# Hash by full-height block-diagonal matmuls, and separate PSUM banks for preparation and output rows

## The chip, the cores and the metric

The kernel runs on one core of one Trainium2 chip. The metric is the device time of one execution in microseconds. The core's engines appear in the profile as PE (TensorE matmuls), PEld (TensorE weight loads), DVE (VectorE), ACT (ScalarE), POOL (GpSimd) and SP (SyncE, which issues transfers). Each engine works through its own instructions in order and waits on semaphores for the others. TensorE writes its results to PSUM, from where VectorE or ScalarE takes them to SBUF.

## The reference

Hash attention comes first, then a gated feed-forward layer with a residual. With batch 4, 8 heads, 768 tokens and a head size of 64:

```python
q_bits = (q @ proj > 0)            # proj is 64 x 6: six bits for each token and head
k_bits = (k @ proj > 0)
mask = bucket(q_bits) == bucket(k_bits)      # a query sees only keys of its bucket
scores = where(mask, q @ k.T / 8, -1e9)
attn = softmax(scores) ;  a = attn @ v

x = a as (4 * 768) tokens x 512
g = x @ w_gate ;  val = x @ w_val            # 512 -> 1536
ffn = (gelu(g) * val) @ w_out                # 1536 -> 512
out = x + sigmoid(x @ w_res) * ffn
```

## The kernel before

Heads are handled in pairs, sixteen of them, and each pair has nine chunks ("slots") of scores. The mask is folded into the scores' matmul: each query and key gets seven more rows, its six bits as plus or minus one half and a constant, and the product of these rows is zero where the buckets agree and a large negative number where they differ. So the hash bits have to be laid out as rows (`bits`), and small transfers (`mask_rows`) put them under the transposed queries and keys (`aug` for the first head of a pair, `second` for the other).

The PSUM pools and the constants of the hash:

```python
    sc_ps = ctx.enter_context(tc.tile_pool(name="sc_ps", bufs=2, space=PSUM))
    av_ps = ctx.enter_context(tc.tile_pool(name="av_ps", bufs=1, space=PSUM))
    mm_ps = ctx.enter_context(tc.tile_pool(name="mm_ps", bufs=1, space=PSUM))
# ... cut ...
    projw = const.tile([P, 2, 32], FP32, name="projw")
    nc.vector.memset(projw, 0.0)
    for a in range(4):
        nc.scalar.dma_start(projw[32 * a:32 * a + 32, :, 0:NBITS],
                            proj.rearrange("(h r) n -> r h n", r=32))
# ... cut: cst, the value that each bit row adds after the comparison ...
```

The hash works on 32x32 blocks (`t32`, transposed by VectorE). A row group `a` of 32 partitions is a tile of the array of its own; one call takes two of the four row groups, for all tensors (`jobs`) of two pairs:

```python
    def hash_mm(jobs, a0, ps=mm_ps, tag="mm"):

        while rows_open:
            mlp_piece()
        hs = ps.tile([P, 2, 512], FP32, tag=tag, name="hs")
        for dh in range(2):
            for j, x in enumerate(jobs):
                for i in range(2):
                    a = a0 + i
                    nc.tensor.matmul(hs[32 * j:32 * j + 32, i, 0:HT * 32],
                                     projw[32 * a:32 * a + 32, dh, :],
                                     t32[x][32 * a:32 * a + 32, :, dh, :],
                                     start=(dh == 0), stop=(dh == 1),
                                     tile_position=(32 * a, 32 * j))
        hsum[a0] = hs
        if a0 == 2:
            for x in jobs:
                del t32[x]

    def hash_bits(jobs, a0):
        n = 32 * len(jobs)
        if a0 == 0:
            bits[jobs[0]] = bit_pool.tile([P, HT, P], BF16, tag="bits", name="bits")
        dst = bits[jobs[0]].rearrange("p c (a n) -> p a c n", a=4)[:n, a0:a0 + 2]
        hs = hsum.pop(a0)[:n, :, 0:HT * 32].rearrange("p a (c n) -> p a c n", c=HT)
        nc.vector.tensor_scalar(dst, hs, 0.0, cst[:n], op0=ALU.is_gt, op1=ALU.add)

    def mask_rows(jobs, xs, eng=nc.sync):
        for j, x in enumerate(jobs):
            if x not in xs:
                continue
            for h, dst in ((1, second[x[0] % NM][x[1]][0:NROW]), (0, aug[x][D:D + NROW])):
                eng.dma_start(dst, bits[jobs[0]][32 * j:32 * j + NROW, h * T:(h + 1) * T])
```

Transposition of queries and keys on TensorE, both sides of a pair in one PSUM tile:

```python
    def transpose_pe(p):
        tp = mm_ps.tile([P, 2, 1024], BF16, tag="mm", name="tp")
        for side in range(2):
            n = nats.pop((p, side)).rearrange("p t h d -> p t (h d)")
            for t in range(T):
                nc.tensor.transpose(tp[:, side, t * P:(t + 1) * P], n[:, t, :], ident)
        tps[p] = tp

    def transposed(x, eng):
        src = tps[x[0]][:, x[1], 0:S]
        dst = new_aug(x).rearrange("p t n -> p (t n)")
        if eng is nc.scalar:
            nc.scalar.copy(dst, src)
        else:
            eng.tensor_copy(dst, src)
```

Values, and the end of a pair. `x_transpose` puts the finished pair into the layout that the feed-forward part reads; it uses TensorE for the first batch and for the last pair of every batch:

```python
    def finish(p):
        b, hp = divmod(p, HP)
        if hp == 0:
            x_tok[b] = x_pool.tile([P, HP, T, 2 * D], BF16, tag="x_tok", name="x_tok")
            x_sb[b] = x_pool.tile([P, HP, T, P], BF16, tag="x_sb", name="x_sb")
        o = av.pop(p)[:, :, 0:T * (D + 1)].rearrange("p h (t d) -> p h t d", t=T)
        rec = sm_pool.tile([P, 2, T], FP32, tag="rec", name="rec")
        nc.vector.reciprocal(rec, o[:, :, :, D])
        nc.vector.tensor_mul(x_tok[b][:, hp].rearrange("p t (h d) -> p h t d", h=2),
                             o[:, :, :, 0:D],
                             rec.unsqueeze(3).to_broadcast([P, 2, T, D]))

    def x_transpose(p):
        b, hp = divmod(p, HP)
        xt = x_tok[b][:, hp]
        if b == 0 or hp == HP - 1:
            while rows_open:
                mlp_piece()
            tp = mm_ps.tile([P, T, P], BF16, tag="mm", name="tp")
            for t in range(T):
                nc.tensor.transpose(tp[:, t, :], xt[:, t, :], ident)
            nc.vector.tensor_copy(x_sb[b][:, hp], tp)
        else:
            nc.sync.dma_start_transpose(out=x_sb[b][:, hp], in_=xt.rearrange("p t n -> p (t n)"))
# ... cut ...
    def values(p, c, e):
        va, vsum = vaug[p]
        if c == 0:
            av[p] = av_ps.tile([P, 2, 512], FP32, tag="av", name="av")
        for hi in range(2):
            o = av[p][:, hi, 0:T * (D + 1)].rearrange("p (t d) -> p t d", t=T)
            if c == 0:
                nc.tensor.matmul(
                    o, eps_sb,
                    vsum[:, hi, 0:D + 1].unsqueeze(1).to_broadcast([P, T, D + 1]),
# ... cut ...
    def flush():
        while pending:
            values(*pending.pop(0))

    def scores(p, c):
        ops = ((D + NROW, aug[p, 0], aug[p, 1]), (P, *second[p % NM]))
        sp = sc_ps.tile([P, 1024], FP32, tag="sp", name="sp")
        for hi, (n, qs, ks) in enumerate(ops):
            off = hi * 512
            for (jt, qt0, nq) in chunks[c]:
                nc.tensor.matmul(sp[:, off:off + nq * P], ks[0:n, jt, :],
                                 qs[0:n, qt0:qt0 + nq, :], start=True, stop=True)
                off += nq * P
        e = e_pool.tile([P, 1024], BF16, tag="e", name="e")
        nc.scalar.activation(e, sp, AF.Exp, scale=float(ALPHA))
        return (p, c, e)
```

Output rows. `rps` (the residual's gate) and `fps` (the feed-forward output) are two halves of one tile of `mm_ps`. It is a generator: each `yield` is the end of a piece that the main loop places between attention slots.

```python
    def project(b, pools=((mm_ps, "mm"),)):

        hh = hidden.pop(b)
        for t in range(T):
            ps, tag = pools[t % len(pools)]
            acc = ps.tile([P, 2, DMODEL], FP32, tag=tag, name="acc")
            rps, fps = acc[:, 0, :], acc[:, 1, :]
            for kk in range(KM):
                nc.tensor.matmul(rps, x_sb[b][:, kk, t, :], wr[:, kk, :],
                                 start=(kk == 0), stop=(kk == KM - 1))
            th = g_pool.tile([P, DMODEL], FP32, tag="th", name="th")
            nc.scalar.activation(th, rps, AF.Tanh, scale=0.5)
            rows_open.append(t)
            yield
            for m in range(KF):
                nc.tensor.matmul(fps, hh[:, m, bass.ts(t, P)], wo[:, m, :],
                                 start=(m == 0), stop=(m == KF - 1))
                if m % 3 == 2 and m < KF - 1:
                    yield
            o = o_pool.tile([P, DMODEL], FP32, tag="o", name="o")
            nc.vector.scalar_tensor_tensor(o, th, 1.0, fps, op0=ALU.add, op1=ALU.mult)
            o3 = o.rearrange("p (k n) -> p k n", k=KM)
            nc.vector.scalar_tensor_tensor(o3, o3, 0.5, x_tok[b][:, :, t, :],
                                           op0=ALU.mult, op1=ALU.add)
            nc.sync.dma_start(out_t[b, t], o)
            rows_open.pop()
            yield
```

The preamble, the schedule of preparation and the main loop:

```python
    jobs0, jobs1 = pair_jobs(0), pair_jobs(1)
    warm_up(8)
    cast((0, 0), nc.scalar)
    cast((0, 1), nc.gpsimd)
    blocks((0, 0))
    blocks((0, 1))
    transpose_pe(0)
    hash_mm(jobs0, 0, sc_ps, "sp")
    hash_mm(jobs0, 2, sc_ps, "sp")
    transposed((0, 0), nc.scalar)
    transposed((0, 1), nc.scalar)
    hash_bits(jobs0, 0)
    hash_bits(jobs0, 2)
    for x in jobs0:
        move_second(x, nc.gpsimd)
    mask_rows(jobs0, jobs0[:1])
    mask_rows(jobs0, jobs0[1:], nc.scalar)
# ... cut: loads, casts, values of pair 0, blocks of pair 1 ...
    at(0, transpose_pe, 1)
    at(0, transposed, (1, 0), nc.vector)
    at(0, transposed, (1, 1), nc.vector)
    at(2, hash_mm, jobs1, 0)
    at(2, move_second, (1, 0), nc.gpsimd)
    at(2, move_second, (1, 1), nc.gpsimd)
    at(2, hash_bits, jobs1, 0)
    at(3, hash_mm, jobs1, 2)
    at(3, hash_bits, jobs1, 2)
    at(3, mask_rows, jobs1, jobs1)
    at(3, values_cast, 1)
    at(3, values_sum, 1)
    at(3, load, 2, (2,))

    for g in range(1, NPAIR // 2):
        s0 = 18 * (g - 1) + (3 if g == 1 else 0)
        pa, pb = 2 * g, 2 * g + 1
        jobs = pair_jobs(pa, pb)
        for i, x in enumerate(jobs):
            at(s0 + 2 * (i // 2), cast, x, nc.gpsimd)
            at(s0 + 1 + i, blocks, x)
        for i, p in enumerate((pa, pb)):
            s1 = s0 + 2 + 3 * i
            if g < 3:
                at(s1, transpose_pe, p)
                for side in range(2):
                    at(s1, transposed, (p, side), nc.vector)
                    at(s1 + 2 + side, move_second, (p, side), nc.gpsimd)
            else:
                for side in range(2):
                    at(s1, transpose_dma, (p, side))
                    at(s1 + 5 + side, move_second, (p, side), nc.gpsimd)
        at(s0 + 8, hash_mm, jobs, 0)
        at(s0 + 8, hash_bits, jobs, 0)
        at(s0 + 10, hash_mm, jobs, 2)
        at(s0 + 10, hash_bits, jobs, 2)
        at(s0 + 11, mask_rows, jobs, jobs[:2])
        at(s0 + 14, mask_rows, jobs, jobs[2:])
        at(s0 + 4, values_cast, pa)
        at(s0 + 4, values_sum, pa)
        at(s0 + 9, values_cast, pb)
        at(s0 + 9, values_sum, pb)
        at(s0 + 5, load, pb, (2,))
        if g + 1 < NPAIR // 2:
            at(s0 + 4, load, pa + 2, (0, 1))
            at(s0 + 6, load, pb + 2, (0, 1))
            at(s0 + 10, load, pa + 2, (2,))
# ... cut: weight loads ...
    LEAD = 5
    HELD = 6
    for s in range(NSLOT):
        p, c = divmod(s, NCH)
        b, slot = divmod(s, NCH * HP)
        new = scores(p, c)
        for f in tasks[s]:
            f()
        if b >= 1:
            if slot < LEAD:
                mlp_piece()
                mlp_piece()
            elif mlp and mlp[0][1] < 5 * T - HELD:
                mlp_piece()
        flush()
        pending.append(new)
        if c == 1 and p >= 1:
            x_transpose(p - 1)
        if b >= 1 and slot == LEAD - 1:
            while mlp:
                mlp_piece()
            gate_val(b - 1)
            mlp.append([project(b - 1), 0])
    flush()
    x_transpose(NPAIR - 1)
    while mlp:
        mlp_piece()
    gate_val(B - 1)
    for _ in project(B - 1, ((mm_ps, "mm"), (av_ps, "av"))):
        pass
```

Of the kernel before, what the change touches and what calls it, by code (L numbers as in the profile page):

```python
# [17 lines left out]
def kernel(  # L18
# [25 lines left out]
    assert D == 64 and S == 768 and NROW <= 32 and HP == KM  # L44
# [29 lines left out]
    mm_ps = ctx.enter_context(tc.tile_pool(name="mm_ps", bufs=1, space=PSUM))  # L74
# [24 lines left out]

    projw = const.tile([P, 2, 32], FP32, name="projw")  # L100
    nc.vector.memset(projw, 0.0)
    for a in range(4):
        nc.scalar.dma_start(projw[32 * a:32 * a + 32, :, 0:NBITS],
                            proj.rearrange("(h r) n -> r h n", r=32))
# [4 lines left out]


    cst = const.tile([P, 1], FP32, name="cst")
    nc.gpsimd.memset(cst, -0.5)
    for j in range(4):
        nc.gpsimd.affine_select(
            out=cst, in_=cst, compare_op=ALU.not_equal,
            fill=(1.0 if j % 2 == 0 else -NBITS / 4.0),
            base=-(32 * j + NBITS), pattern=[[0, 1]], channel_multiplier=1)
# [3 lines left out]
                            base=0, pattern=[[-1, P]], channel_multiplier=1)  # L121

# [27 lines left out]
    wps = av_ps.tile([P, 512], FP32, tag="av", name="wps")  # L150

    def warm_up(n):
        for _ in range(n):
            nc.tensor.matmul(wps, eps_sb, warm, start=True, stop=True)
# [28 lines left out]
    def transpose_pe(p):  # L183
        tp = mm_ps.tile([P, 2, 1024], BF16, tag="mm", name="tp")
        for side in range(2):
            n = nats.pop((p, side)).rearrange("p t h d -> p t (h d)")
            for t in range(T):
                nc.tensor.transpose(tp[:, side, t * P:(t + 1) * P], n[:, t, :], ident)
        tps[p] = tp

    def transposed(x, eng):
        src = tps[x[0]][:, x[1], 0:S]
        dst = new_aug(x).rearrange("p t n -> p (t n)")
        if eng is nc.scalar:
            nc.scalar.copy(dst, src)
        else:
            eng.tensor_copy(dst, src)
# [7 lines left out]
    mlp, rows_open = [], []  # L205
# [11 lines left out]
    def hash_mm(jobs, a0, ps=mm_ps, tag="mm"):  # L217

        while rows_open:
            mlp_piece()  # L220
        hs = ps.tile([P, 2, 512], FP32, tag=tag, name="hs")
        for dh in range(2):
            for j, x in enumerate(jobs):
                for i in range(2):
                    a = a0 + i
                    nc.tensor.matmul(hs[32 * j:32 * j + 32, i, 0:HT * 32],  # L226
# [321 lines left out]
```

## Time and profile before

| | |
|---|---|
| time, median of 2 runs | 434.26 us (432.81 to 435.72) |
| profiled run | 430.43 us, span 428.6 us, granted TensorE clock 0.982 |
| exp on ScalarE (L339) | 144 of 1022 ns |
| hash matmuls on TensorE (L226) | 512 records, 27.7 us busy |
| bits on VectorE (L242) | 18, 18.2 us busy |
| output rows on TensorE (L375, L382) | 25.4 and 72.6 us busy |
| gate and value projections (L354) | 125.5 us busy |

The span begins with a preamble that ends with the first score matmul at 15.65 us. Attention alone follows (the first batch), then four times a stage of gate and value projections (L354), and between them stages in which the next batch's attention is mixed with the output rows of the batch before. The last 28 us are the output rows of the last batch. A group in the profile is named by line, engine and tile: `acc` is the rows' PSUM tile, `hs` the hash sums, `tp` transposes, `sp` scores, `av` the values' output, `e` the exponentials, `th` the tanh, `o` the output row in SBUF. "idle before" is the time in which the engine stood still ahead of that group and what ended it. FP32 matmuls are recorded as two passes each.

### The profile page before, as it was taken

Reading aid. Unit: us, or ns where it says so; the run is one execution under the profiler, and the core shown is the slowest. Engines: PE = TensorE matmul, PEld = TensorE weight load, DVE = VectorE, ACT = ScalarE, POOL = GpSimd, SP = SyncE. Lnnn points to the kernel's source line nnn. Section 1 sums busy time; section 2 is a strip of 40 time slices with the busy share of each in tenths; the row PEclk is TensorE's granted clock in tenths of the full one; section 3 lists DMA queues with packets and bytes.
Section 4 is the critical chain, followed back from the end, with each engine's and each line's share of the span. In section 5 each row is a group of like instructions: output and inputs, shape, how many; then the busy total and the mean of one; then the engine's idle time right before and its main releaser. Section 6 shows DMA issues by size and latency. Waiting matters only on the chain. (4 is left out here: it accounts for less than half of the span.)

```text
span 428.6 us, 7961 instructions
## 1 busy us (share of the span) xinstructions
PE 367.1 (86%) x3301; PEld 202.5 (47%) x3360; DVE 154.1 (36%) x201; ACT 208.6 (49%) x227; POOL 108.1 (25%) x187
## 2 busy tenths in 40 slices
PE   7688788999789887999779988999869976999884
PEld 3354544665335444566335544566435543566431
DVE  3472634333232434433331543433241212333232
ACT  3366768335327765533537765633626784233110
POOL 4969596133011154250002145230000000000000
PEclk9999999999799999999999999999998998999999
DMA  7343989980030590900012490700020100000011
GB/s 257 116 139 131 263 125 192 213 192 0 26 84 29 132 255 24 262 4 2 24 55 60 111 274 8 136 0 2 2 65 29 52 18 26 24 2 0 26 63 59
DMA packets 47299, 37.32 MB, mean 87 GB/s; under 512 B 25312, under 2 KB 44192, under 8 KB 47264
## 3 DMA queue, kind: packets, MB, share of 16 engines
q1 hardware_dynamic: 40308, 31.15, 26.4%
q0 software_dynamic: 6336, 5.24, 8.3%
q8 instruction: 26, 0.43, 0.4%
q10 hardware_dynamic: 620, 0.42, 0.3%
q14 instruction: 9, 0.07, 0.1%
HBM read 29.37 MB, written 6.29 MB: 83 GB/s over the span
## 5 line engine op out<-in xcount | busy, mean ns | idle before, releaser
L339 ACT ACTIVATE e<-sp 128x1024 bf16<-128x1024 f32 x144 | 143.7, 1022 | 66.9 <-PE sp L335 58.5
L382 PE MATMUL acc<-wo,hh 128*128 128x512 bf16 x275 | 72.6, 388 | 9.5 <-ACT th L378 8.4
L360 ACT ACTIVATE gt<-sp 128x768 bf16<-128x768 f32 x48 | 38.9, 810 | 82.4 <-PE sp L354 82.3
L316 PEld LDWEIGHTS <-e 128*128 128x128 bf16 x1152 | 51.8, 98 | 54.7 <-ACT e L339 34.9
L363 DVE TENSOR_TENSOR hh<-gt,sp 128x768 bf16<-128x768 bf16 x48 | 45.8, 955 | 82.0 <-PE sp L354 82.0
L316 PE MATMUL av<-va,e 128*128 128x65 bf16 x1152 | 62.3, 195 | 13.4 <-ACT e L339 12.3
L354 PE MATMUL sp<-x_sb,wg 128*128 128x256 bf16 (+1 forms) x378 | 69.9, 325 | 0.3
L354 PE MATMUL sp<-x_sb,wv 128*128 128x512 bf16 (+1 forms) x374 | 69.7, 324 | 0.5
L335 PE MATMUL sp<-aug,aug 71*128 71x512 bf16 x192 | 55.6, 330 | 4.5 <-DMA aug<-bits 4.5
L382 PEld LDWEIGHTS <-hh 128*128 128x128 bf16 x288 | 28.4, 99 | 44.0 <-issue 17.8
L354 PEld LDWEIGHTS <-wg 128*128 128x128 bf16 x384 | 37.3, 98 | 25.0 <-issue 0.5
L354 PEld LDWEIGHTS <-wv 128*128 128x128 bf16 x384 | 37.4, 98 | 24.4
L335 PE MATMUL sp<-second,second 128*128 128x256 bf16 (+1 forms) x171 | 47.5, 323 | 0.0
L387 DVE SCALAR_TENSOR_TENSOR o<-th,acc 128x512 f32<-128x512 f32 x24 | 16.4, 684 | 79.4 <-PE acc L382 60.8
L179 POOL COPY second<-aug 64x768 bf16<-64x768 bf16 x32 | 25.8, 826 | 66.3 <-DMA aug<-nat 57.9
L378 ACT ACTIVATE th<-acc 128x512 f32<-128x512 f32 x24 | 14.3, 596 | 57.7 <-PE acc L375 57.4
L254 POOL CAST va<-ldv 128x768 bf16<-128x768 f32 x16 | 13.2, 827 | 101.4 <-DMA ldv<-in_v_dram 74.1
L226 PE MATMUL hs<-t,projw 32*32 32x384 f32 x512 | 27.7, 509 | 7.9 <-DVE o L387 6.7
L375 PE MATMUL acc<-wr,x_sb 128*128 128x512 bf16 x88 | 25.4, 393 | 9.5 <-DVE bits L242 7.0
L284 DVE RECIPROCAL rec<-av 128x12 f32<-128x12 f32 x16 | 3.7, 232 | 75.6 <-PE av L316 75.6
L201 DVE STREAM_TRANSPOSE t<-ld 128x768 f32<-128x768 f32 x32 | 29.3, 952 | 2.2 <-DMA ld<-in_q_dram 2.2
L242 DVE TENSOR_SCALAR bits<-hs,cst 128x768 bf16<-128x768 f32 (+1 forms) x18 | 18.2, 1015 | 23.5 <-PE hs L226 23.5
(45 smaller groups left out, 219.9 us busy)
## 6 DMA issues: line engine op xcount, KB each, us to landing
ld<-in_q_dram SPq DMA_DIRECT2D x16, 384.0 KB
ldv<-in_v_dram SPq DMA_DIRECT2D x16, 384.0 KB
out_dram<-o SPq DMA_DIRECT2D x24, 256.0 KB
ld<-in_k_dram SPq DMA_DIRECT2D x15, 384.0 KB
wg<-in_moe_w_gate_dram POOLq DMA_DIRECT2D x4, 384.0 KB, 5.7
wv<-in_moe_w_val_dram POOLq DMA_DIRECT2D x4, 384.0 KB, 7.0
wo<-in_moe_w_out_dram POOLq DMA_DIRECT2D x3, 512.0 KB, 17.8
wr<-in_moe_w_res_dram POOLq DMA_DIRECT2D x1, 512.0 KB, 11.1
```

Of the source, the lines that this page charges most:

```text
L179: eng.tensor_copy(second[x[0] % NM][x[1]][D:P], aug[x][D:P])
L201: nc.vector.transpose(tt.rearrange("p c h n -> p (c h n)"), raw[x].rearrange("p c d -> p (c d)"))
L226: nc.tensor.matmul(hs[32 * j:32 * j + 32, i, 0:HT * 32], projw[32 * a:32 * a + 32, dh, :], t32[x][32 * a:32 * a + 32, :, dh, :], start=(dh ...
L242: nc.vector.tensor_scalar(dst, hs, 0.0, cst[:n], op0=ALU.is_gt, op1=ALU.add)
L316: nc.tensor.matmul(o[:, qt, :], e[:, off:off + P], va[:, hi, jt, 0:D + 1], start=False, stop=(jt == T - 1), skip_group_check=True)
L335: nc.tensor.matmul(sp[:, off:off + nq * P], ks[0:n, jt, :], qs[0:n, qt0:qt0 + nq, :], start=True, stop=True)
L339: nc.scalar.activation(e, sp, AF.Exp, scale=float(ALPHA))
L354: nc.tensor.matmul(sp[:, c0:c1], w[:, kk, bass.ts(m, P)], xs[:, kk, c0:c1], start=(kk == 0), stop=(kk == KM - 1))
L360: nc.scalar.activation(gt, sp[:, 0:S], AF.Gelu)
L363: nc.vector.tensor_mul(hh[:, m, :], gt, ps[1][:, 0:S])
L375: nc.tensor.matmul(rps, x_sb[b][:, kk, t, :], wr[:, kk, :], start=(kk == 0), stop=(kk == KM - 1))
L382: nc.tensor.matmul(fps, hh[:, m, bass.ts(t, P)], wo[:, m, :], start=(m == 0), stop=(m == KF - 1))
```

## The change

The hash matmul takes the full 128 partitions at once: `projw` becomes block-diagonal, so that the four row groups of a tensor come out as 4 x 6 rows of one result (`hs`). That result is compared and brought to SBUF once (`hb`), and matmuls with a constant selection matrix (`sel`) then put each bit into its row and add the constant row (`spread`, three per group of pairs). It is meant to shorten the hash on TensorE.

The two banks of `mm_ps` become one bank for everything of preparation (`tp_ps`: transposes, hash, spread, and the residual's gate `rps`) and one for output rows (`row_ps`: `fps`). With this, a hash or transpose no longer has to wait until a row is complete, and the rule that completes it first (`rows_open`) goes. Transposes are made for one side at a time. The store of a row is issued after the next row's first piece, so that loads and small transfers are not queued behind it. In the slot c = 1 the values are not flushed; the new pair's first values are computed one slot later. Loads of `v` are placed earlier.

```diff
-    mm_ps = ctx.enter_context(tc.tile_pool(name="mm_ps", bufs=1, space=PSUM))
+    tp_ps = ctx.enter_context(tc.tile_pool(name="tp_ps", bufs=1, space=PSUM))
+    row_ps = ctx.enter_context(tc.tile_pool(name="row_ps", bufs=1, space=PSUM))
 ...
-        nc.scalar.dma_start(projw[32 * a:32 * a + 32, :, 0:NBITS],
+        nc.scalar.dma_start(projw[32 * a:32 * a + 32, :, NBITS * a:NBITS * (a + 1)],
 ... cut: cst goes, sel (128 x 4 x 4 x 32, bf16) comes ...
-    def transpose_pe(p):
-        tp = mm_ps.tile([P, 2, 1024], BF16, tag="mm", name="tp")
+    def transpose_pe(x):
+        tp = tp_ps.tile([P, T, P], BF16, tag="tp", name="tp")
 ... cut: hash_mm and its two calls of hash_bits go ...
+    def hash_bits(jobs):
+        n = 32 * len(jobs)
+        hs = tp_ps.tile([P, HT, 32], FP32, tag="tp", name="hs")
+        for dh in range(2):
+            for j, x in enumerate(jobs):
+                nc.tensor.matmul(hs[32 * j:32 * j + 32], projw[:, dh, :], t32[x][:, :, dh, :],
+                                 start=(dh == 0), stop=(dh == 1), tile_position=(0, 32 * j))
+        hb = bit_pool.tile([P, HT, 32], BF16, tag="hb", name="hb")
+        nc.vector.tensor_scalar(hb[:n], hs[:n], 0.0, 0.5, op0=ALU.is_gt, op1=ALU.subtract)
+        bits[jobs[0]] = (hb, bit_pool.tile([P, HT, P], BF16, tag="bits", name="bits"))
+
+    def spread(jobs, i, pool=None, eng=None):
+        n = 32 * len(jobs)
+        hb, dst = bits[jobs[0]]
+        pool, tag = pool or (tp_ps, "tp")
+        sp = pool.tile([P, 4, 4, 32], FP32, tag=tag, name="spr")
+        for a in range(4):
+            nc.tensor.matmul(sp[:n, :, a, :],
+                             sel[:n, a].rearrange("p j n -> p (j n)")[:, 0:n],
+                             hb[:n, 4 * i:4 * i + 4, :], start=True, stop=True)
+        dst = dst[:n, 4 * i:4 * i + 4, :]
+        src = sp[:n].rearrange("p c a n -> p c (a n)")
+        ... copied by ScalarE (eng) or VectorE ...
 ...
-            while rows_open:
-                mlp_piece()
-            tp = mm_ps.tile([P, T, P], BF16, tag="mm", name="tp")
+            tp = tp_ps.tile([P, T, P], BF16, tag="tp", name="tp")
 ...
-    def project(b, pools=((mm_ps, "mm"),)):
+    def project(b, pools=((row_ps, "row"),)):
         hh = hidden.pop(b)
+        store = None
         for t in range(T):
-            ps, tag = pools[t % len(pools)]
-            acc = ps.tile([P, 2, DMODEL], FP32, tag=tag, name="acc")
-            rps, fps = acc[:, 0, :], acc[:, 1, :]
+            rps = tp_ps.tile([P, DMODEL], FP32, tag="tp", name="rps")
 ...
             nc.scalar.activation(th, rps, AF.Tanh, scale=0.5)
-            rows_open.append(t)
             yield
+            if store:
+                nc.sync.dma_start(*store)
+            ps, tag = pools[t % len(pools)]
+            fps = ps.tile([P, DMODEL], FP32, tag=tag, name="fps")
 ...
-            nc.sync.dma_start(out_t[b, t], o)
-            rows_open.pop()
+            store = (out_t[b, t], o)
             yield
+        nc.sync.dma_start(*store)
 ... the preamble: ...
-    transpose_pe(0)
-    hash_mm(jobs0, 0, sc_ps, "sp")
-    hash_mm(jobs0, 2, sc_ps, "sp")
+    transpose_pe((0, 0))
     transposed((0, 0), nc.scalar)
+    hash_bits(jobs0)
+    spread(jobs0, 0, (row_ps, "row"))
+    spread(jobs0, 1, (av_ps, "av"), nc.scalar)
+    spread(jobs0, 2)
+    transpose_pe((0, 1))
     transposed((0, 1), nc.scalar)
-    hash_bits(jobs0, 0)
-    hash_bits(jobs0, 2)
 ... pair 1: transposed one side ahead of slot 0, one in it; hash in slot 1, spread in 2, 3, 4, mask rows in 4 ...
 ... later groups: ...
+                sx = s0 + 2 + i
+                at(sx, transpose_pe, x)
+                at(sx, transposed, x, nc.vector)
+                at(sx + 1, move_second, x, nc.gpsimd)
-        at(s0 + 8, hash_mm, jobs, 0)
-        at(s0 + 8, hash_bits, jobs, 0)
-        at(s0 + 10, hash_mm, jobs, 2)
-        at(s0 + 10, hash_bits, jobs, 2)
+        at(s0 + 7, hash_bits, jobs)
+        for i in range(3):
+            at(s0 + 8 + i, spread, jobs, i)
 ... cut: v loads move to earlier slots ...
-        flush()
+        if c != 1:
+            flush()
 ...
-    for _ in project(B - 1, ((mm_ps, "mm"), (av_ps, "av"))):
+    for _ in project(B - 1, ((row_ps, "row"), (av_ps, "av"))):
```

The warm-up matmuls write a tile of `sc_ps` instead of one of `av_ps`.

## The prediction

> **What bounds the kernel now.** I read the page's busy shares first, then the waits of TensorE, then a table of stages, then TensorE's timeline inside one stage of each kind.
>
> ```profile
> PE 367.1 (86%) x3301; PEld 202.5 (47%) x3360; DVE 154.1 (36%) x201; ACT 208.6 (49%) x227; POOL 108.1 (25%) x187
> ...
> PE av L316 <- ACT e L339: 12.3, 28, 0.7
> PE acc L382 <- ACT th L378: 8.4, 12, 0.8
> PE acc L375 <- DVE bits L242: 7.0, 6, 1.2
> PE hs L226 <- DVE o L387: 6.7, 8, 0.9
> PE tp L297 <- DVE o L387: 2.9, 3, 1.3
> ```
>
> TensorE is the only engine near its limit, and about 61 us of the span it is idle. A wait line gives the waiter, what released it, the sum, the count and the longest. Four of the five lines are one thing: tiles of `mm_ps`, a single buffer of two banks, handed from row to hash to row to transpose. Only the first line is ScalarE really being the slower side.
>
> ```profile
> 15.65:71.97 56.32, 45.49 (x673) 26.68 (x684) 28.00 (x40) 39.55 (x41) 44.77 (x73) 1.00 0.75 172
> ...
> 204.20:270.50 66.30, 55.20 (x605) 29.20 (x614) 24.86 (x34) 39.53 (x43) 14.70 (x26) 1.00 0.33 93
> 270.50:302.10 31.60, 31.39 (x203) 19.03 (x204) 10.98 (x12) 12.10 (x15) 6.02 (x10) 1.00 0.20 33
> ...
> 398.00:428.60 30.60, 21.59 (x95) 9.14 (x94) 9.23 (x13) 3.58 (x6) 0.00 (x0) 0.97 0.14 52
> ```
>
> Columns: window, its length, then busy us of TensorE, weight loads, VectorE, ScalarE, GpSimd, then granted clock, DMA share, GB/s. The second window is attention mixed with output rows (three of this kind: 103.55 to 172.6, 204.2 to 270.5, 302.1 to 366.8), the third is the gate/value projection (TensorE solid, nothing to gain), the last is the closing rows. In the first, attention alone, GpSimd is at 80%.
>
> ```profile
> 209.66 1.24 PE L382 MATMUL acc<-wo,hh 128*128 128x512 bf16 x5
> ...
> 211.73 1.52 PE L226 MATMUL hs<-t,projw 32*32 32x384 f32 x32 [0.84 <-DVE o L387]
> 214.43 1.02 PE L375 MATMUL acc<-wr,x_sb 128*128 128x512 bf16 x4 [1.18 <-DVE bits L242]
> ```
>
> Here TensorE waits for the row's eviction, hashes for 1.52 us, then waits for the bits: 2.0 us lost round one half-hash. In the closing rows:
>
> ```profile
> 399.51 2.75 PE L382 MATMUL acc<-wo,hh 128*128 128x512 bf16 x12 [0.69 <-ACT th L378]
> 402.09 1.03 PE L375 MATMUL acc<-wr,x_sb 128*128 128x512 bf16 x4
> ...
> 403.81 2.75 PE L382 MATMUL acc<-wo,hh 128*128 128x512 bf16 x12 [0.69 <-ACT th L378]
> ```
>
> A row takes 403.81 - 399.51 = 4.30 us; its 12 matmuls take (402.09 - 399.51)/12 = 0.215 us each, and 16 of those would be 3.44. The rest is the wait for tanh, because both halves of a row are one tile.
>
> ```profile
> 7.31 3.41 PE L226 MATMUL hs<-t,projw 32*32 32x384 f32 x32
> ...
> 12.21 1.34 ACTq L249 DMA_DIRECT2D second<-bits  x1
> ...
> 15.65 0.38 PE L335 MATMUL sp<-aug,aug 71*128 71x512 bf16 x1 [3.53 <-DMA aug<-bits]
> ...
> 22.21 0.84 POOL L164 TENSOR_SCALAR nat<-ld 128x768 bf16<-128x768 f32 x1
> 22.99 0.83 POOL L166 CAST nat<-ld 128x768 bf16<-128x768 f32 x1
> ```
>
> At the start one chain (hash, bits, small transfers) sets the first score at 15.65. GpSimd's cast of pair 2 ends just as TensorE's transposes need it at 23.74: no slack there.
>
> **What the skill says.** "TensorEngine Tiling (Array Packing)", section Tiling Modes, lists 128x32 with four independent tiles beside 32x32 with sixteen, and says that a change of mode drains the array. The trace agrees as far as it goes: 32 hash matmuls (eight tiles) take 1.52 us and 16 (four tiles) 1.49, so column tiles do run side by side; full-height ones no run shows yet. "TensorE: Matmul & The Clock Gate", section Back-to-back issue gap, has 134 cycles for 128 columns (56 ns); the trace has six transposes of 128 columns in 0.33 us, 55 ns each. "PSUM — Partial Sum Buffer", Specifications, gives eight banks of 512 FP32 values. Before: 4 score, 2 value, 2 shared. After: 4, 2, one `tp`, one `row`. So nothing is added; the shared pair is split by purpose, and everything of preparation now meets in one bank.
>
> **The change, part by part.**
>
> *Hash.* A half-hash moves TensorE on by 1.46 us (31.93 to 33.39). A group of four tensors had two, 2.92; at full height it has 2 halves of depth x 2 passes (the 512 records are twice the 256 matmuls of the code), four rounds as before, but once: 1.46. The four row groups of a tensor are now summed in one instruction because `projw` is block-diagonal, so a group falls from 64 records to 16. Added are three spreads, each four 128-column matmuls at 55 ns plus a little for weights: 0.25 (an estimate from the transposes). 2.92 becomes 2.2 per group: -0.7, nine groups, about -6 in all where TensorE binds. VectorE: two bits of 1.02 become one of 384 elements (about 0.6, by its 768 in 1.02) and three copies of 512 (about 0.73): 2.0 becomes 2.8, harmless at 36%.
>
> *Mixed stages (66.3 us).* Waits of TensorE that disappear in this window: hash on row 2.5, row on bits 2.4, `fps` on tanh 1.5, transpose on row 0.8, row on row 0.4, together 7.6. Hash work, two groups: 5.84 to 4.4, -1.4. Forced row-finishing also spent the row pieces early, so that about 13 slots near the end had none; those run at ScalarE's pace, 1.03 against 0.69 us of TensorE (0.44 scores, 0.25 values). With pieces spread one per slot seven remain: 6 x 0.34 = -2.0. New: rows and preparation share `tp`. A row's first part comes every fifth slot; by the slot numbers it meets a spread in slot 10 and a hash in slot 25, each costing drain 0.2, copy 0.6 to 0.7, a semaphore: about 0.9; the next spread may wait on tanh: 0.2 to 0.5. Together +2.5. Net -8.5; I book -7 for each of two stages, since TensorE's waits partly hide in others' queues. The third has one group of pairs: waits -6.5, hash -0.7, slots -2.0, new +1.5 (the last `x_transpose` still waits for `x_tok`, 1.2); booked -6.5. Sum -20.5.
>
> *Closing rows.* Halves in two tiles: 6 x (4.30 - 3.44) = -5.2. Booked -5.
>
> *Start.* Worse. Four rounds at the cold clock (0.64 us apart in the first hash) remain about 2.6, now after the first transposes left `tp` (7.6): hash to 10.4, bits 0.6, spread matmuls 0.6, two VectorE copies to 13.2 (the third on ScalarE), only then side 1's transposes, ScalarE's copy to 14.5, GpSimd's move to 15.4, then ScalarE's transfer, landing 1.3 later: first score at 17.5 to 18 against 15.65, +2. The move shifts GpSimd's queue too. It had run 9.96 to 25.4 with 0.4 of slack; its cast of pair 2 would now end at 15.4 + 12.9 = 28.3 (12.9 is today's queue from 9.96 to 23.3 less its 0.4 gap: two casts, pair 0's values, four fills, two moves, pair 1's values, the cast), and TensorE, in order, needs it in slot 5, by then due at about 24: slot 5 ends some 4 us later than now.
>
> *Attention alone.* Regained: 4 half-hashes of g = 1, 2 become 2, about -1 each by ScalarE's idle time of 1.2 at such slots: -2; transposes of one side per slot instead of two: -1.5; slot c = 1 no longer runs the new pair's values between `x_tok` and the next scores: -0.56 x 3; new meetings in `tp` (slots 10, 28) +1.8; a one-us wait on a mask transfer maybe gone. About -4, so start plus attention is 0 (-3 to +3).
>
> *Stores and loads.* Late stores free the SP queue (two stores held it 8.5 us from 133.42), but what stood behind them shows no wait on TensorE: 0.
>
> Sum: 0 - 20.5 - 5 = -25.5 from 434.3, 409. Since waits that I haven't listed only add, I say 411.
>
> **Rivals.** (1) `tp` is the new queue: every hash, spread, transpose and row goes through it, and each meeting costs 0.9. If four more per stage hit, three stages lose 11: about 420. For it: one buffer. Against: slot numbers rarely coincide. (2) The start grows by more than the booked 4 because of GpSimd's queue and TensorE standing still behind it: 415 to 418. For it: 80% and no slack. (3) Full-height column tiles do not overlap: a group then takes four times 1.3, 5.2 us, seven full groups lose about 27 against my sum: about 436, no gain. Against: column tiles overlap today. (4) ScalarE becomes the bound of the mixed stages: 36 x 1.03 + 3.6 = 41 us against 58 predicted, so no. (5) All waits really go: 403.
>
> **Range and chances.** The firm parts (tail, bits and row waits) give about -18 alone; the start may take back 4 more. 402 to 423 holds 8 in 10. Slower than 425.6 needs rival 3 or two of the others together: faster 0.85, same 0.10, slower 0.05.
>
> **What would show it.** Right: hash groups of 8 or 16 instructions per group in 1.5 us; no wait of `hs` or `acc` on VectorE's `o`; closing rows at 3.45; `rps` waiting about 0.9 on `spr` or `hb` copies once or twice per stage; mixed stages of 57 to 60. Start: first score near 17.7, and transposes in slot 5 waiting for `nat`. Wrong: hash busy over 20 us; many `tp` waits; mixed stages over 63; a first score after 19.

## The result, and the profile after

The changed kernel takes 405.18 us (404.84 to 405.53, two runs) against 434.26 before: a ratio of 0.933, 95% interval 0.919 to 0.947. Run again beside the experiments it took 403.35 us, ratio 0.929 (0.923 to 0.935). The profiled span went from 428.6 to 403.5 us, 25.1 less; the medians differ by 29.1, since the profiled execution of the kernel before, 430.43 us, lies 3.8 below its median.

First the page's busy shares and the waits of TensorE, as they were read for the kernel before:

```profile
PE 360.7 (89%) x3029; PEld 209.1 (52%) x3084; DVE 158.3 (39%) x218; ACT 209.7 (52%) x228; POOL 109.6 (27%) x186
...
PE rps L377 <- DVE bits L247: 7.5, 3, 2.6
PE av L319 <- ACT e L342: 7.2, 19, 0.7
PE sp L338 <- DMA aug<-bits: 3.1, 1, 3.1
...
PE rps L377 <- DVE hb L229: 1.4, 2, 0.7
```

Of the four waits for a tile of `mm_ps`, three are gone: hash on row, `fps` on tanh, transpose on row. The fourth, row on bits, is back in another tile: `rps` waits three times some 2.5 us for the copy of a spread and twice 0.7 for `hb`, 8.9 us in all, against six waits with 7.0 us before. Scores wait 3.1 us for mask rows. The same view of the kernel before has two such waits, the first score's of 3.5 and one of 1.0:

```profile
PE sp L335 <- DMA aug<-bits: 4.5, 2, 3.5
```

Then the table of stages (window, length, busy us of TensorE, weight loads, VectorE, ScalarE, GpSimd, granted clock, DMA share, GB/s):

```profile
20.60:82.30 61.70, 50.27 (x584) 30.88 (x592) 29.19 (x45) 40.30 (x41) 46.27 (x76) 0.89 0.65 144
...
204.00:261.40 57.40, 52.04 (x535) 29.83 (x542) 25.80 (x38) 39.76 (x43) 16.85 (x28) 1.00 0.46 108
261.40:292.90 31.50, 31.29 (x204) 19.09 (x205) 11.08 (x12) 11.94 (x15) 4.42 (x8) 1.00 0.13 19
...
377.70:403.50 25.80, 20.82 (x96) 9.34 (x96) 9.23 (x13) 3.58 (x6) 0.00 (x0) 0.97 0.16 62
```

Each stage is bounded by the first score or gate matmul that begins it:

| stage | before, us | after, us | difference |
|---|---|---|---|
| start, to the first score | 15.7 | 20.6 | +4.9 |
| attention alone | 56.3 | 61.7 | +5.4 |
| first mixed stage | 69.1 | 58.9 | -10.2 |
| second mixed stage | 66.3 | 57.4 | -8.9 |
| third mixed stage | 64.5 | 53.7 | -10.8 |
| four gate projections | 125.9 | 125.5 | -0.4 |
| closing rows | 30.8 | 25.8 | -5.0 |

So 35 us came out of the mixed stages, projections and closing rows, and 10 were lost ahead of them. TensorE's timeline in the second mixed stage and in the closing rows shows both halves of the gain, and a new wait:

```profile
207.19 1.50 PE L224 MATMUL hs<-t,projw 128*32 128x384 f32 x16
208.62 0.82 PE L387 MATMUL fps<-wo,hh 128*128 128x512 bf16 x3
...
213.07 0.38 PE L239 MATMUL spr<-hb,sel 128*128 128x128 bf16 x4
216.01 1.02 PE L377 MATMUL rps<-wr,x_sb 128*128 128x512 bf16 x4 [2.56 <-DVE bits L247]
...
378.60 2.75 PE L387 MATMUL fps<-wo,hh 128*128 128x512 bf16 x12
381.19 1.03 PE L377 MATMUL rps<-wr,x_sb 128*128 128x512 bf16 x4
382.06 2.75 PE L387 MATMUL fps<-wo,hh 128*128 128x512 bf16 x12
```

The hash of a group of four tensors is one block of 16 records in 1.50 us, in the middle of a row, with no wait around it. In slot 10 `rps` waits 2.56 us. A closing row takes 382.06 - 378.60 = 3.46 us, where it had taken 4.30.

The start, from the timeline of all engines:

```profile
8.31 2.78 PE L224 MATMUL hs<-t,projw 128*32 128x384 f32 x8 [1.43 <-DMA projw<-in_proj_dram]
...
13.20 0.68 DVE L247 CAST bits<-spr 64x512 bf16<-64x512 f32 x1 [0.17 <-PE spr L239]
...
15.72 0.43 SPq L89 DMA_DIRECT2D ldv<-in_v_dram  x1
16.21 0.59 SPq L89 DMA_DIRECT2D ld<-in_q_dram  x1
...
16.60 0.73 ACTq L254 DMA_DIRECT2D aug<-bits  x1
...
17.43 0.82 PE L191 MATMUL tp<-ident,nat 128*128 128x128 bf16 x6 [2.70 <-POOL nat L168]
...
20.37 0.10 PEld L338 LDWEIGHTS <-aug 71*128 71x128 bf16 x1 [0.46 <-DMA aug<-bits]
...
20.61 0.63 PE L338 MATMUL sp<-aug,aug 71*128 71x512 bf16 x1
```

In the kernel before the end of the start was:

```profile
13.63 0.73 ACTq L249 DMA_DIRECT2D aug<-bits  x1
...
13.96 0.43 SPq L88 DMA_DIRECT2D ldv<-in_v_dram  x1
...
15.62 0.10 PEld L335 LDWEIGHTS <-aug 71*128 71x128 bf16 x1 [3.99 <-issue]
```

The first score waits for its last mask rows. They were issued 3.0 us later than before (16.60 against 13.63), and they took longer: the weight load that needs them began 3.8 us after the issue (20.37), where it had begun 2.0 after (15.62). Before, they were issued ahead of the load of `v`, 384 KB; now the loads of `v` and of a query stand ahead of them. Meanwhile TensorE does pair 1's transposes, late for want of a cast, and the warm-up matmuls, about 0.43 us each.

### The profile page after: what moved, and what is told of

Its sections match the earlier page's. It is cut to its first block, busy times and chain, and to the rows that moved or that the text cites. A ratio compares the mean times of both kernels' runs of the same rounds, so it can differ in the third digit from the quotient of the medians.

```text
span 403.5 us, 7430 instructions
## 1 busy us (share of the span) xinstructions
PE 360.7 (89%) x3029; PEld 209.1 (52%) x3084; DVE 158.3 (39%) x218; ACT 209.7 (52%) x228; POOL 109.6 (27%) x186
## 5 line engine op out<-in xcount | busy, mean ns | idle before, releaser
L342 ACT ACTIVATE e<-sp 128x1024 bf16<-128x1024 f32 x144 | 144.8, 1023 | 60.5 <-PE sp L338 52.2
L363 ACT ACTIVATE gt<-sp 128x768 bf16<-128x768 f32 x48 | 38.9, 810 | 80.2 <-PE sp L357 80.2
L387 PE MATMUL fps<-wo,hh 128*128 128x512 bf16 x272 | 71.6, 381 | 1.5 <-issue 0.5
L357 PE MATMUL sp<-x_sb,wv 128*128 128x256 bf16 (+1 forms) x376 | 69.8, 325 | 0.4
L357 PE MATMUL sp<-x_sb,wg 128*128 128x512 bf16 (+1 forms) x376 | 69.8, 325 | 0.4
L338 PE MATMUL sp<-aug,aug 71*128 71x512 bf16 x192 | 57.1, 338 | 3.1 <-DMA aug<-bits 3.1
L338 PE MATMUL sp<-second,second 128*128 128x256 bf16 (+1 forms) x174 | 49.9, 332 | 0.0
L392 DVE SCALAR_TENSOR_TENSOR o<-th,fps 128x512 f32<-128x512 f32 x24 | 16.4, 685 | 65.2 <-ACT e L342 32.1
L377 PE MATMUL rps<-wr,x_sb 128*128 128x512 bf16 x92 | 25.7, 395 | 9.2 <-DVE bits L247 7.5
L380 ACT ACTIVATE th<-rps 128x512 f32<-128x512 f32 x24 | 14.3, 595 | 34.8 <-PE rps L377 29.4
L247 DVE CAST bits<-spr 128x512 bf16<-128x512 f32 (+1 forms) x26 | 17.9, 687 | 17.3 <-PE spr L239 17.3
L259 POOL CAST va<-ldv 128x768 bf16<-128x768 f32 x16 | 13.2, 825 | 41.9 <-PE av L319 41.3
L338 PEld LDWEIGHTS <-aug 71*128 71x128 bf16 x192 | 16.8, 99 | 7.5 <-DMA aug<-bits 3.7
L338 PEld LDWEIGHTS <-second 128*128 128x128 bf16 x192 | 19.3, 100 | 2.1
```

What stands on the lines that cost most here:

```text
L247: nc.vector.tensor_copy(dst, src)
L338: nc.tensor.matmul(sp[:, off:off + nq * P], ks[0:n, jt, :], qs[0:n, qt0:qt0 + nq, :], start=True, stop=True)
L357: nc.tensor.matmul(sp[:, c0:c1], w[:, kk, bass.ts(m, P)], xs[:, kk, c0:c1], start=(kk == 0), stop=(kk == KM - 1))
L363: nc.scalar.activation(gt, sp[:, 0:S], AF.Gelu)
L377: nc.tensor.matmul(rps, x_sb[b][:, kk, t, :], wr[:, kk, :], start=(kk == 0), stop=(kk == KM - 1))
L387: nc.tensor.matmul(fps, hh[:, m, bass.ts(t, P)], wo[:, m, :], start=(m == 0), stop=(m == KF - 1))
```

## The experiments

All are edits of the changed kernel, each timed in several rounds beside the kernel before. Stage lengths are from their profiles; line numbers shift by up to three.

### The changed kernel again

> The changed kernel unchanged, as the reference for the runs beside it. Expected 405 us, within 1 us; first score at 20.6 us of the span and the first gate matmul at 82.3.

Measured: 403.35 us, ratio 0.929 (0.923 to 0.935); first score at 20.3, attention alone 61.9, first gate matmul at 82.3. The median is 1.65 us under the expected 405. The stage lengths of the two profiles agree within 0.3 us, but both are of executions that took 405.5; the four times here differ by up to 2.7, so a stage that differs by 1 or 2 us in one profile shows little.

### Start: no second warm-up

```diff
-    warm_up(6)
```

> The six warm-up matmuls ahead of the first score are left out. Theory A (in the changed kernel TensorE, in order, runs them after the late transposes of pair 1, so they stand on the path): the first score moves from 20.6 to about 18.5, the first gate matmul by about 1.5 to 2 with it, time 403 to 404. Rival B (the start does not set the end of attention alone; the mask transfer of slot 18 does): the first score moves but the gate matmul stays at 82, time 405. Rival C (without them the clock stays low for the first slots): time 405 to 406.

Measured: 404.71 us, ratio 0.932 (0.926 to 0.937). The first score came at 19.2 and the gate matmul at 80.2, the numbers of theory A, but not for its reason. The run with early stores (below) keeps the warm-ups, and its first score came at 19.36. The weight load of the first score, without the warm-ups:

```profile
19.23 0.10 PEld L338 LDWEIGHTS <-aug 71*128 71x128 bf16 x1 [2.30 <-DMA aug<-bits]
```

With early stores and all warm-ups:

```profile
19.36 0.10 PEld L338 LDWEIGHTS <-aug 71*128 71x128 bf16 x1 [0.53 <-DMA aug<-bits]
```

Both wait for the last mask rows, issued at 15.53 and 15.52. That is 0.8 us earlier than in the changed kernel's repeat (16.32), because the first hash took 1.98 and 1.99 us there instead of 2.78. So the warm-ups cost the first score no more than about 0.1 us. The scores then ran at half the clock (0.61 us for 512 columns, where 0.38 is usual), but so they do in the changed kernel (0.63). The second mixed stage was 1.5 us longer, with the clock at half for 3.4 us, and the time was not shorter.

### Start: no bank waits for another

```diff
 ... cut: transpose_pe and hash_bits take a pool ...
-    transposed((0, 0), nc.scalar)
-    hash_bits(jobs0)
-    spread(jobs0, 0, (row_ps, "row"))
-    spread(jobs0, 1, (av_ps, "av"), nc.scalar)
-    spread(jobs0, 2)
-    transpose_pe((0, 1))
-    transposed((0, 1), nc.scalar)
+    transpose_pe((0, 1), (av_ps, "av"))
+    hash_bits(jobs0, (row_ps, "row"))
+    transposed((0, 0), nc.scalar)
+    transposed((0, 1), nc.scalar)
+    spread(jobs0, 0)
+    spread(jobs0, 1, (sc_ps, "sp"), nc.scalar)
+    spread(jobs0, 2, (sc_ps, "sp"))
```

(and without the second warm-up)

> As the run without warm-up, and at the start side 1 of pair 0 is transposed at once into the bank of the values, the hash goes to the row bank, the spreads to tp and the two score tiles, so nothing of the start waits for another's bank. Theory A (the serial order in one tp bank, and GpSimd's queue shifted by it, made the start late): first score at 15.5 to 16.5, GpSimd's cast of pair 2 ends about 6 us earlier (29.2 to 23), first gate matmul at 76 to 78, time 399 to 401. Rival B (mask transfers and their clock dip set the first gate matmul): gate matmul at 81 to 82, time 404 to 405.

Measured: 402.19 us, ratio 0.924 (0.917 to 0.931). First score at 17.2, GpSimd's cast of pair 2 begins at 23.3 instead of 28.1, gate matmul at 76.5: theory A in kind, with a smaller gain at the first score than its 15.5 to 16.5. The last mask rows were issued at 15.17, again ahead of the load of `v` (15.49), and the weight load that waits for them began at 17.14, 2.0 us after. Of the 5.7 us gained by the first gate matmul only 2.5 were left at the end of the span: this profile's second and third mixed stages were 1.6 us longer each, with more slices below full clock. The wait for the mask rows in slot 18 stayed at 3.3.

### Attention alone: weight loads later

```diff
-    for s in (20, 22, 28, 30, 36, 37, 38, 39):
+    for s in (25, 26, 31, 32, 36, 37, 38, 39):
         at(s, load_w)
```

> Only the issue of the first weight loads moves, from slots 20, 22, 28, 30 to 25, 26, 31, 32. Theory A (the 3.1 us wait of the scores of slot 18 for the mask rows comes from the weight load that GpSimd issued at 43.9 us, just ahead of the last mask transfer at 44.3): the wait falls under 1 us, no half clock from 48 to 56 us, first gate matmul 3 to 6 us earlier, time 400 to 402. Rival B (the bits are simply late: spread of slot 13 and four issues of 0.7 us each): the wait stays at 2.5 to 3.2 us, time 404 to 406.

Measured: 397.42 us, ratio 0.914 (0.909 to 0.920), better than the 400 to 402 expected. The wait is 0.7 us, attention alone 55.0 instead of 61.9, the clock full from 21.3 us on:

```profile
43.14 0.69 SPq L254 DMA_DIRECT2D aug<-bits  x1
...
43.93 0.39 SPq L89 DMA_DIRECT2D ldv<-in_v_dram  x1
...
45.09 0.39 PE L338 MATMUL sp<-aug,aug 71*128 71x512 bf16 x1 [0.68 <-DMA aug<-bits]
```

Rival B falls: the issue came only a microsecond earlier, the v load was still right behind the mask rows, and yet they landed in time.

How fine the race is shows in other runs. In the changed kernel (repeat) GpSimd's weight load is issued before the last mask rows of pair 2:

```profile
43.65 0.97 POOL L153 DMA_DIRECT2D wg<-in_moe_w_gate_dram  x1
44.16 0.69 SPq L254 DMA_DIRECT2D aug<-bits  x1
...
48.74 0.61 PE L338 MATMUL sp<-aug,aug 71*128 71x512 bf16 x1 [3.31 <-DMA aug<-bits]
```

In the kernel whose values are flushed in slot 1 (below) the same two issues are 0.06 us apart:

```profile
43.65 0.97 POOL L153 DMA_DIRECT2D wg<-in_moe_w_gate_dram  x1
43.71 0.69 SPq L254 DMA_DIRECT2D aug<-bits  x1
...
45.67 0.10 PEld L338 LDWEIGHTS <-aug 71*128 71x128 bf16 x1 [0.81 <-DMA aug<-bits]
```

A transfer of 10.5 KB lands 2.0 us after its issue when that is 0.06 us behind the weight load's, and 4.6 after it when it is half a microsecond behind. The kernel with early stores lies between: 0.35 us apart, landing after 3.7, wait 2.5.

### Attention alone: TensorE kept busy through the wait

```diff
+        if s == 17:
+            fill = tp_ps.tile([P, 512], FP32, tag="tp", name="fill")
+            for _ in range(14):
+                nc.tensor.matmul(fill, eps_sb, warm, start=True, stop=True)
```

> The changed kernel with 14 idle matmuls of 512 columns (3.0 us, their result is not used) put ahead of the scores of slot 18, where TensorE otherwise stands still for the mask rows. Theory A (of the 6.9 us that the late mask rows cost attention alone, 61.9 against 55.0 us, about 3 are the wait and the rest the halved clock that follows the idle stretch): the mask rows come as late as before, the clock of the slices after it stays at full, attention alone 57 to 59 us, time 399 to 402. Rival B (the clock falls anyway, or its fall costs nothing because ScalarE sets the pace): attention alone 60.5 to 63 us, time 403 to 406.

Measured: 399.84 us, ratio 0.923 (0.920 to 0.926), attention alone 57.1, the clock full. The issues are 0.33 us apart (43.66 and 43.99), and the scores begin at 48.12, as soon as the filling is done, so that the landing itself is not seen. The same window in the repeat of the changed kernel,

```profile
44.00:48.00 4.00, 1.17 (x20) 0.74 (x19) 0.00 (x0) 1.87 (x2) 0.62 (x1) 0.85 0.77 86
48.00:52.00 4.00, 2.79 (x17) 1.39 (x18) 1.71 (x3) 1.86 (x2) 0.00 (x0) 0.50 1.00 309
```

and with the filling matmuls:

```profile
44.00:48.00 4.00, 3.74 (x31) 1.90 (x28) 0.00 (x0) 1.70 (x2) 0.63 (x1) 1.00 0.75 85
48.00:52.00 4.00, 2.74 (x31) 1.67 (x30) 2.52 (x4) 2.61 (x3) 0.00 (x0) 1.00 1.00 320
```

The clock column is the difference, 0.50 against 1.00: TensorE is busy equally long and gets 31 matmuls done instead of 17. So of the 6.9 us that the late mask rows cost (61.9 - 55.0) an estimated 4.8 (61.9 - 57.1) are the clock, and 2.1 the wait; the 4.8 hold 0.6 us by which the scores began earlier here (48.12 against 48.74). The ratio's interval just overlaps that of the changed kernel (0.923 to 0.935), but its four times, 399.25 to 400.94, all lie below the other four.

### The hash twice over

```diff
-        for dh in range(2):
+        for dh in (0, 1, 0, 1):
```

> The changed kernel with every hash done twice over into the same bank (the second pass overwrites the first). Theory A (a group of four tensors at full height is worth one pass, 1.3 us, of TensorE, and where TensorE binds it comes whole into the time): each full group's hash rises from 1.5 to 2.8 us, the three mixed stages grow by 2.6, 2.6 and 1.3 (2, 2 and 1 groups), attention alone by 1 to 3, time 411 to 413 against 403 to 405. Rival B (the hash hides beside the waits, so its shortening brought little): the mixed stages grow by less than 1 each, time 405 to 407.

Measured: 415.9 us, ratio 0.955 (0.947 to 0.962), above the 411 to 413 expected. The mixed stages grew by 2.7, 4.2 and 1.4 us (the second includes some 1.5 of a lower clock, as it had without the warm-up). One pass of a group is 1.3 us of TensorE and arrives whole in the mixed stages: theory A. Attention alone grew by only 0.3, but there the clock was at half for 6.8 us after the mask rows instead of 10.2; the start grew by 1.8.

### The banks shared again

```diff
-            rps = tp_ps.tile([P, DMODEL], FP32, tag="tp", name="rps")
+            ps, tag = pools[t % len(pools)]
+            acc = ps.tile([P, 2, DMODEL], FP32, tag=tag, name="acc")
+            rps, fps = acc[:, 0, :], acc[:, 1, :]
 ... transposes, hash and spread in mm_ps too; hash, spread and x_transpose each after:
+        while rows_open:
+            mlp_piece()
```

> The changed kernel with one shared buffer of two banks again for transposes, hash, spread and rows, both halves of a row in one tile, and the rule that completes an open row before a hash, spread or transpose; the new hash and the late stores stay. Theory A (the split of the banks carries the gain of the mixed stages and of the closing rows): mixed stages of 66 to 72 us instead of 58.9, 57.4, 53.7, closing rows 30.8 instead of 25.8, time 430 to 440. Rival B (the shorter hash carries it): mixed stages within 3 us of the changed kernel's, only the closing rows 5 us longer, time 410 to 415.

Measured: 447.01 us, ratio 1.028 (1.020 to 1.036). Mixed stages 70.9, 70.9 and 67.6 us, closing rows 30.8; the time is above the 430 to 440 expected. TensorE's waits in the second mixed stage:

```profile
PE acc L384 <- DVE bits L250: 2.8, 3, 0.9
PE spr L242 <- DVE o L398: 2.5, 3, 0.8
PE acc L393 <- ACT th L387: 1.9, 4, 0.8
```

With the new hash in the old bank the kernel is slower than before the change, since there are now four visits to the bank per group instead of two, each with its handover. This is the clearest reading of the study: the split of the banks carries the gain, and the new hash with the other parts of the change, but in shared banks, is a loss.

### Values of slot 0 not deferred

```diff
-        if c != 1:
-            flush()
+        flush()
```

> Only the values of slot c = 0 are computed in slot c = 1 again. Theory A (the deferral saves about half a microsecond at each change of pair where ScalarE binds, and nothing in the mixed stages): attention alone 1 to 3 us longer, mixed stages within 1 us, time 405 to 407. Rival B (the deferral is neutral because x_transpose waits for x_tok in the same slot anyway): within 1 us of the changed kernel.

Measured: 402.30 us, ratio 0.925 (0.919 to 0.932), not distinguishable from the changed kernel. Attention alone was 56.3, shorter instead of longer, because the mask rows won their race (shown above); the mixed stages were 0.7 and 2.5 longer, 0.2 shorter, and the second had its clock at half for 3.4 us. What the deferral is worth by itself stays open.

### Stores at once, and loads of v where they were

```diff
-            store = (out_t[b, t], o)
+            nc.sync.dma_start(out_t[b, t], o)
```

> Only the stores of output rows are issued at once again, as in the kernel before. Theory A (the late stores free the SP queue, but nothing behind them is waited for by TensorE): time within 1 us of the changed kernel, 402 to 405. Rival B (loads and mask rows of the mixed stages are queued behind the stores): mixed stages 1 to 3 us longer, time 406 to 410.

Measured: 403.45 us, ratio 0.931 (0.927 to 0.935); mixed stages 59.1, 57.4, 53.8. The late stores are worth nothing that can be measured: theory A. Start and attention alone were 4.3 us shorter in this profile, by the first hash and the mask rows (both above); the median shows none of it.

```diff
-    at(5, load, 3, (2,))
 ...
+        at(s0 + 5, load, pb, (2,))
-            at(s0 + 8, load, pa + 2, (2,))
-            at(s0 + 12, load, pb + 2, (2,))
+            at(s0 + 10, load, pa + 2, (2,))
```

> Only the loads of v go back to the slots of the kernel before. Theory A (in attention alone the last mask rows of pair 2 land late when the weight load of GpSimd is issued before them, 43.65 against 44.16 us, and early when it is not; v has no part in it): the wait of slot 18 stays at about 3 us unless the order of these two issues turns, mixed stages as in the changed kernel, time 402 to 406. Rival B (the v load issued right behind the mask rows makes them late): the wait falls under 1 us with the order unchanged, time 396 to 399.

Measured: 398.84 us, ratio 0.919 (0.915 to 0.924; one of the four executions, 406.72 us at a lower granted clock, is left out of the ratio). Attention alone is 55.2 us and the wait of slot 18 is 0.6, but the order did turn: GpSimd's cast of values now waits 3.0 us for v, so that its queue comes to the weight load at 46.63 only, after the mask rows (44.28). By itself this run cannot part the theories; with the run of late weight loads, where v stayed behind the mask rows, it can. The earlier v loads did harm here, by bringing GpSimd's weight load ahead of the mask rows.

### Two better versions

The first joins the start in banks of its own (warm-ups kept) with the later weight loads and moves hash, spread and mask rows of later groups one slot earlier:

```diff
-        at(s0 + 7, hash_bits, jobs)
+        at(s0 + 6, hash_bits, jobs)
 ... spread at s0 + 7 + i, mask_rows at s0 + 10 and s0 + 13
```

> Changed kernel with three moves: start in banks of its own with the warm-up matmuls kept, weight loads three to five slots later, hash, spread and mask rows of later groups one slot earlier. The last is for the 2.56 us wait in slot 10: there the third spread's copy stands in VectorE's queue behind the end of a pair and an output row. Theory A: start 17.2 or a little less, attention alone 52 to 54, first two mixed stages 55 to 56, time 389 to 392. Rival B (with the spreads one slot earlier the wait only moves to another slot): mixed stages stay at 57 to 59, time 393 to 396.

Measured: 390.46 us, ratio 0.897 (0.892 to 0.903). Start 17.0, attention alone 54.9 (52 to 54 expected), mixed stages 56.6, 56.5, 52.2. The wait of 2.56 us is gone from slot 10, but 1.3 us appear in slot 25, where a spread now meets a row's first part, and 0.7 where the hash of slot 6 waits for tanh: the time is as theory A had it, the first two mixed stages between the theories.

The second moves the transposes of finished pairs one slot on, into the idle row bank in the first batch, and keeps spreads out of slot 25:

```diff
-        if c == 1 and p >= 1:
+        if c == 2 and p >= 1:
             x_transpose(p - 1)
 ...
-            tp = tp_ps.tile([P, T, P], BF16, tag="tp", name="tp")
+            pool, tag = (row_ps, "row") if b == 0 and hp < HP - 1 else (tp_ps, "tp")
 ... for even g > 2: hash at s0 + 5, first spread at s0 + 6
```

> The best version so far, and: x_transpose one slot later, in the first batch through the row bank, which is idle there; in each mixed stage the second group's hash and first spread one slot earlier, so that no spread falls in slot 25 with a row's first part. Theory A: the waits of attention alone for x_tok (3.4 us) and for the bits (1.3) go, attention alone 51 to 53 instead of 54.9; in the first two mixed stages the 1.3 us wait of a row for the bits goes, 55.3 instead of 56.5; time 385 to 388. Rival B (where ScalarE sets the pace in attention alone these waits hide behind it): attention alone stays at 54 to 55, time 388 to 390.

Measured: 385.61 us, ratio 0.891 (0.888 to 0.894), the fastest of all: about 4% under the changed kernel by their ratios (0.891 / 0.929 = 0.959). Start 16.2, mixed stages 55.3, 55.2, 52.0: theory A there. Attention alone gained 1.3 us, between the theories.

## Why the prediction was right or wrong

The time lay in the range and the direction was right. The sum of the steps, -25.5, is even the -25.1 of the span, but only because two errors of about 10 us cancelled.

**Closing rows.** Booked -5, measured -5.0, by the mechanism named: two tiles, no wait for tanh.

**The hash at full height.** Predicted were 1.46 us per group, from its start to that of the next work; measured 1.43 (207.19 to 208.62) in 16 records; column tiles do overlap, and the rival that doubted it falls. Three spreads cost 0.22 us of TensorE each (predicted 0.25). The doubled hash shows such work arriving whole in the mixed stages.

**Mixed stages.** The itemised sums were -8.5, -8.5 and -7.7; I booked -7, -7 and -6.5 "since TensorE's waits partly hide in others' queues". This discount is the step that failed: measured were -10.2, -8.9 and -10.8, and the run with shared banks brought the waits back. The discount was 4.2 us of the 9.4 that were missing. The second stage, at full clock before and after, is within 0.4 of its sum. In the other two the clock rose from 0.95 to 0.97 of full. Counted as lost time that is an estimated 1.7 us (0.05 x 69.1 - 0.03 x 58.9) and 1.6, which leaves -8.5 and -9.2. Waits of the values that the sum had left out are in these figures too: in the third stage those for `e` fell from 2.7 to 1.4 us and those for `x_tok`, whose line (4.9 us over the span) the prediction's list of waits skips, from 1.3 to none.

**New meetings in tp.** Two per stage at about 0.9 were predicted, +2.5 with a wait on tanh. There are two in each of the first two mixed stages, in the slots named; slot 25 costs 0.68 and slot 10 costs 2.56. The mis-sized term is the copy: I gave it a free VectorE. VectorE's timeline in slot 10 of the first mixed stage:

```profile
122.37 0.69 DVE L392 SCALAR_TENSOR_TENSOR o<-th,fps 128x512 f32<-128x512 f32 x1
123.09 0.84 DVE L394 SCALAR_TENSOR_TENSOR o<-o,x_tok 128x512 f32<-128x512 f32 x1
123.86 0.22 DVE L289 RECIPROCAL rec<-av 128x12 f32<-128x12 f32 x1
124.11 0.96 DVE L290 TENSOR_TENSOR x_tok<-av,rec 128x768 bf16<-128x768 f32 x1
124.99 0.68 DVE L247 CAST bits<-spr 128x512 bf16<-128x512 f32 x1
```

The spread's matmuls were done at about 123.2; their copy began at 124.99, behind a finished row and a finished pair. An engine that is idle for most of the span is still a queue where a bank's release has to pass through it.

**Start and attention alone.** Booked 0 (-3 to +3), measured +10.3: the prediction's largest error. Up to the move of side 1 the chain of the start was right in kind and nearly in size (bits complete at 13.9, said 13.2; the move ended at 16.5, said 15.4; the cast of pair 2's first side ended at 29.2, said 28.3, from a queue read to 23.3 where the trace before has that cast ending at 23.05). The step that failed is the last one, ScalarE's transfer, "landing 1.3 later": it was issued at once, and the weight load that waits for it began 3.9 us after the move. The two terms said, 15.4 and 1.3, also make 16.7 and not the 17.5 to 18 given. The order of issue was left out. In the four profiles in which the last mask rows of the start were issued ahead of the load of `v` (the kernel before, the run with the start's banks apart and the two better versions) the first score's weight load began 2.0 us after their issue; in the ten with the load of `v` ahead of them, 3.7 to 4.0. No run moved that order alone, so this cause is read from the traces and not shown by an experiment. TensorE standing still for pair 2's cast in slot 5 hardly showed (0.3 us), because TensorE itself was not there earlier.

For attention alone, -2 from the first score on is what my +2 and 0 imply; with the weight loads later it was 55.0 against 56.3, -1.3, close to that. What I had no term for is the 6.9 us on top: the mask rows lost their race with a weight load, and the clock halved in the idle stretch. I had even noted a wait of 1.0 us at that place before the change, and booked it as "maybe gone".

"TensorE: Matmul & The Clock Gate", section What's actually happening, says that TensorE falls to half clock after an idle window of about 3.4 us. Here less was enough. In the changed kernel (repeat) the clock fell 1.4 us after the last work at 45.43 and stayed low through 8.3 us of work:

```profile
45.43:46.80 1.37, 0.00 (x1) 0.00 (x0) 0.00 (x0) 0.44 (x1) 0.00 (x0) 1.00 0.85 60
46.80:48.74 1.94, 0.00 (x0) 0.01 (x1) 0.00 (x0) 0.00 (x0) 0.00 (x0) 0.50 1.27 233
48.74:57.00 8.26, 7.79 (x60) 5.23 (x61) 4.10 (x7) 3.74 (x4) 0.82 (x1) 0.50 0.61 188
```

With the wait filled it did not fall. In the first mixed stage of the changed kernel it fell 2.1 us into the wait of 2.56 (four `rps` matmuls took 1.67 us instead of 0.86), and in the second, with the same wait, not: the length alone doesn't decide.

**Stores and loads.** The stores were worth 0, as predicted. The loads of v, also put at 0, were not: in attention alone they cost 6.7 us by way of GpSimd's queue (61.9 against 55.2), the same time that the later weight loads win back.

## What to carry to other kernels

Give a PSUM bank to one kind of work when work of several kinds meets in it: the handovers of a shared bank cost TensorE more here than the matmuls that were saved. When the change lets another engine run ahead, look for what that engine starts next and which transfers it will overtake; a small transfer that a matmul waits for belongs well ahead of any large load. Count an idle stretch of TensorE of some 3 us at more than its length.

## What the runs showed of the hardware

A 10.5 KB transfer issued 0.5 us after a 384 KB weight load from GpSimd's queue landed about 4.6 us after its issue; issued 0.35 us after it, about 3.7; issued 0.06 us after it, 2.0. At the start such a transfer took 3.7 to 4.0 us behind 384 KB loads and 2.0 ahead of them.

In an idle stretch of 3.3 us TensorE's clock went to 0.50 after 1.4 us and stayed there for 10.2 (46.8 to 57.0), 8.3 of them with work; a second stretch followed (67.3 to 70.7). Together they cost an estimated 4.8 us, against 2.1 for the wait itself.

Full-height 32-column FP32 tiles run side by side like 32x32 ones: 16 records of 128 x 32 weights and 384 columns took 1.50 us, 8 records 1.49, where 32 and 16 records of 32x32 took 1.52 and 1.49 in the kernel before.
